# One fused attention, expert and feed-forward kernel: when two weight matrices are converted, and how the second layer's first product sits in PSUM

## The chip, the cores and the metric

The kernel runs on one core of a Trainium2 chip. The metric is device microseconds (us) of that core from start to end of the program. A core has TensorE (matmuls, called PE in the profile, with its weight loads as PEld), VectorE (DVE), ScalarE (ACT), GpSimd (POOL) and SyncE (SP, which here only issues DMAs). SBUF is the on-chip working memory; PSUM, where matmuls write, has eight banks of 2 KB per partition.

## The reference

Three stages follow each other. The test data are random draws.

```python
# 1. attention, 2 batches x 8 heads, 768 positions, 64 wide: scores only within equal cluster
mask = q_assign[:, :, :, None] == k_assign[:, :, None, :]      # nearest centroid of 16, per head
scores = np.where(mask, 0.125 * (q @ k.T), -1e9)
x = softmax(scores) @ v                                        # -> 1536 tokens x 512
# 2. mixture of experts, 8 experts, one expert per token: the first layer
e_idx = np.argmax(x @ w_gate + modality_bias[modality_id], axis=1)
h = np.maximum(x[mask] @ w1[e], 0.0)                           # 512 -> 1024
out[mask] = gate_w[mask, None] * (h @ w2[e])                   # 1024 -> 512
# 3. dense feed-forward: the second layer
h = x @ w_in                                                   # 512 -> 2048, w_in is float64
g = h * np.tanh(log1p(exp(h)))                                 # mish
return (g @ w_out).astype(np.float32)                          # 2048 -> 512, w_out is float64
```

## The kernel before

Every product is made of three float16 matmuls (high by high, high by low, low by high part), so each operand must be split in a high and a low float16 part. [...] One chunk (`conv_chunk`, L1021 to L1035) is a 512 KB load, three integer operations on VectorE that shift the bits of a double into those of a float (L1027, L1028, L1030), one ScalarE copy to float16 (L1033), and one VectorE operation for the low part (L1035). `convs` (L1039) does the 16 chunks as a generator of steps: six empty ones, then four for each chunk, after the third of which it issues the load of the chunk after next (two load buffers, `RAWB`).

The program is written as such generators: `attention()` for the 16 heads, `moe1()` for the first layer (`M`), `gate(0)` and `gate(1)` for routing and sorting the tokens of a batch, `convs("i")` and `convs("o")`, `h_units(q)` and `o_units(q)` for the first and second product of the second layer over a sixth of the tokens (a third of one batch, 256 tokens). The first layer takes each batch in two slots (the two most common experts), and each slot in eight pieces: four of `w1`, whose results are `hT` (L963 to L969), four of `w2`, whose results are `x1` (L978 to L993). `h_units` needs `x1` of its batch and `win`; `mish` (L1095) turns four of its 16 column blocks at a time into `g` (ScalarE: sigmoid, arctan, sin; VectorE multiplies by the product that still lies in PSUM, L1110; ScalarE and GpSimd split the result, L1113 and L114); `o_units` needs `g` and `wout`.

While attention is emitted, steps of the other generators are put between its steps: from step 163 on, one step of `convs("i")` at every second one (`CI1 = 2`, L1302), unless batch 0 is being gated, and the first layer at a set pace (L1307). Then what is left of `convs("i")` is emitted at once (L1315). After that three calls of `mix` share out the rest: `mix` always takes a step of the part that has done the smallest fraction of the length it is given. The first mix (L1328) has the second slot of batch 0, `gate(1)` with a length of 40, the first 20 steps of `convs("o")` and `h_units(0)`; the second (L1329) the first slot of batch 1, `h_units(1)` and all the rest of `convs("o")`; the third (L1331) the last slot, and all products that remain.

A scheduler then orders the instructions of PE, DVE, ACT and POOL by its own estimate of times, within what the data allow; each engine executes its list in order. SyncE's list is kept in the order in which the program is written. So every load that SyncE issues stands behind the wait of the load before it.

In PSUM the second layer's first product has two tiles of two banks, each holding four column blocks (`h_t[q]`, L1131); its second product has two tiles of a bank, and two banks are shared by the rest.

## Time and profile before

| | us |
|---|---|
| median of 3 runs (689.56 to 696.43) | 689.66 |
| the profiled execution | 697.58 |
| its span, first to last instruction | 695.9 |
| PE busy, share of the span | 616.7, 89% |
| DVE busy | 400.6, 58% |
| ACT busy | 459.3, 66% |
| POOL busy | 294.9, 42% |

Shares over the whole span hide the stages. The profile is read in stretches, and their limits are events: the twelfth head's output leaves VectorE at 233.0, the sixteenth's at 320.6; the first `hT` after attention is done at 324.0, the last `x1` of batch 1's first slot at 451.6; the last matmul ends at 687.8. A matmul's end is modelled, and PE counts as busy while short matmuls overlap, so busy PE is not PE at its peak. A VectorE record overlaps the next by some 0.08 us; busy times count that once.

### The profile page before, as it was taken

How to read it: one execution, taken by the hardware profiler on the slowest of the kernel's cores; microseconds unless marked ns; L12 is line 12 of the kernel's file. 1: busy time of each engine (PE TensorE's matmuls, PEld its weight loads, DVE VectorE, ACT ScalarE, POOL GpSimd, SP SyncE). 2: the span in 40 equal slices, each digit the busy share in tenths (PEclk: the TensorE clock that was granted, in tenths of full speed). 3: DMA queues.
4: the chain of work that ended last, by engine and by line, in shares of the span. 5: the costliest groups of instructions: out<-in, count | busy, mean ns of one | idle time of the engine just before them, and what ended most of it. 6: DMA issues, size and time to landing. Idle time of an engine off the chain costs nothing.

```text
span 695.9 us, 14026 instructions
## 1 busy us (share of the span) xinstructions
PE 616.7 (89%) x5618; PEld 409.6 (59%) x5619; DVE 400.6 (58%) x751; ACT 459.3 (66%) x699; POOL 294.9 (42%) x251
## 2 busy tenths in 40 slices
PE   1698999987589988987999889999999999999995
PEld 1365867756356645554766556666666667667542
DVE  6768767689699899999858888823121110110100
ACT  2587998875678767765677678846554476776500
POOL 5577888796776744551141211111311212313211
PEclk9999999989789999999999999999999999999999
DMA  7532372312853234346445544321100000000000
GB/s 229 139 74 64 87 206 53 87 41 61 273 162 102 68 97 121 123 128 189 135 158 183 183 150 161 113 61 31 47 16 1 15 16 1 31 1 31 2 31 34
DMA packets 56743, 64.43 MB, mean 93 GB/s; under 512 B 10080, under 2 KB 46944, under 8 KB 56672
## 3 DMA queue, kind: packets, MB, share of 16 engines
q1 hardware_dynamic: 42064, 48.74, 24.1%
q10 hardware_dynamic: 12688, 8.42, 4.0%
q0 software_dynamic: 1920, 6.32, 2.4%
q8 instruction: 46, 0.75, 0.5%
q14 instruction: 25, 0.20, 0.1%
HBM read 46.23 MB, written 6.32 MB: 76 GB/s over the span
## 4 chain that ended last, share of the span: by engine, by line
PE 40%; DVE 28%; issue 10%; ACT 9%; DMA 7%; SPq 3%; POOL 1%; ACTq 0%; POOLq 0%; DVEq 0%
PE h L1007 12%; PE o L1159 12%; PE eps L1007 6%; DVE f L1028 4%; DVE mxh L351 3%; DVE f L1030 3%; PE s L391 2%; DVE w L922 2%; DMA QK<-hl 2%; DVE f L1027 2%; DMA QK<-oT 2%; DVE win L1035 2%; DVE mxh L356 1%; DVE dg L702 1%; PE eps L273 1%
## 5 line engine op out<-in xcount | busy, mean ns | idle before, releaser
L114 POOL TENSOR_TENSOR el<-e,eh 128x768 f16<-128x768 f32 x86 | 146.0, 1709 | 63.9 <-ACT eh L400 42.9
L1007 PE MATMUL h<-x,win 128*128 128x256 f16 x1152 | 133.3, 273 | 3.2 <-ACT s L1103 2.4
L1007 PEld LDWEIGHTS <-win 128*128 128x128 f16 x1152 | 112.5, 98 | 24.1 <-issue 4.7
L1110 DVE SCALAR_TENSOR_TENSOR s<-s,h 128x1024 f32<-128x1024 f32 x24 | 29.3, 1222 | 167.4 <-ACT s L1108 164.8
L1007 PEld LDWEIGHTS <-w 128*128 128x128 f16 x768 | 75.2, 99 | 67.6 <-issue 12.1
L114 POOL TENSOR_TENSOR xb<-s,xb 128x1024 f16<-128x1024 f32 x18 | 39.6, 2201 | 142.7 <-ACT xb L1113 142.5
L1159 PE MATMUL o<-wout,xb 128*128 128x512 f16 x432 | 96.8, 379 | 0.0
L391 PE MATMUL s<-QK 128*128 128x384 f16 x320 | 80.2, 346 | 9.6 <-ACT e L393 9.2
L393 ACT ACTIVATE e<-s 128x384 f32<-128x384 f32 x152 | 70.0, 489 | 24.5 <-PE s L391 19.3
L1007 PE MATMUL eps<-xw,w 128*128 128x416 f16 x384 | 76.8, 349 | 8.7 <-DVE hT L969 3.2
L400 ACT ACTIVATE eh<-e 128x768 f16<-128x768 f32 x88 | 74.3, 848 | 2.5 <-PE s L391 1.3
L351 DVE TENSOR_REDUCE mxh<-x 128x1 f32<-128x512 f32 x96 | 64.6, 680 | 17.2 <-PE x L350 17.1
L1103 ACT ACTIVATE s<-h,cst 128x512 f32<-128x512 f32 x48 | 32.8, 686 | 61.8 <-PE h L1007 61.5
L1007 PE MATMUL eps<-hT,w 128*128 128x416 f16 x384 | 71.6, 339 | 0.7 <-DVE hT L969 0.7
L1159 PEld LDWEIGHTS <-xb 128*128 128x128 f16 x432 | 42.3, 98 | 47.6
L429 PE MATMUL av<-vst,el 128*128 128x65 f16 x528 | 61.3, 197 | 5.8 <-POOL el L114 5.8
L427 PE MATMUL av<-vst,eh 128*128 128x65 f16 x528 | 63.8, 198 | 1.9 <-DVE xt L442 1.6
L428 PE MATMUL av<-vst,eh 128*128 128x64 f16 x528 | 63.8, 199 | 0.0
L429 PEld LDWEIGHTS <-el 128*128 128x128 f16 x528 | 51.3, 102 | 15.5 <-POOL el L114 11.3
L427 PEld LDWEIGHTS <-eh 128*128 128x128 f16 x528 | 51.5, 100 | 9.1 <-DVE xt L442 2.6
L391 PEld LDWEIGHTS <-QK 128*128 128x128 f16 x384 | 35.3, 103 | 33.3 <-issue 20.6
L428 PEld LDWEIGHTS <-eh 128*128 128x128 f16 x528 | 51.4, 101 | 3.3 <-issue 0.3
(224 smaller groups left out, 1053.4 us busy)
## 6 DMA issues: line engine op xcount, KB each, us to landing
wf<-in_moe_w_dram ACTq DMA_DIRECT2D x16, 512.0 KB
raw<-in_moe_w_in_dram SPq DMA_DIRECT2D x16, 512.0 KB
raw<-in_moe_w_out_dram SPq DMA_DIRECT2D x16, 512.0 KB
wf<-in_moe_w_dram SPq DMA_DIRECT2D x16, 512.0 KB
QK<-hl SPq DMA_DIRECT2D x32, 192.0 KB
xs<-dr SPq DMA_DIRECT2D x12, 258.0 KB
t<-in_k_dram SPq DMA_DIRECT2D x8, 384.0 KB
t<-in_q_dram SPq DMA_DIRECT2D x8, 384.0 KB
```

Of the source, the lines that this page charges most:

```text
L114: nc.gpsimd.tensor_tensor(out=out_, in0=in0, in1=in1, op=ALU.subtract)
L351: nc.vector.reduce_max(out=mx_t[i][:, t, 0:1], in_=sp, axis=AX.X)
L391: nc.tensor.matmul(sps[hf][:, 0:HS], lhsT=st[:, KA + a, kt * P:(kt + 1) * P], rhs=st[:, QA + a, hf * HS:(hf + 1) * HS], start=(a == 0), st ...
L393: nc.scalar.activation(out=e32[:, hf * HS:(hf + 1) * HS], in_=sps[hf][:, 0:HS], func=AF.Exp, scale=1.0 / float(D) ** 0.5)
L400: nc.scalar.activation(out=eh, in_=e32, func=AF.Copy)
L427: nc.tensor.matmul(av[:, t, :], lhsT=eh[:, cols], rhs=vs[:, h, 0:NV], start=(kt == 0 and t == 0), stop=False, skip_group_check=True)
L428: nc.tensor.matmul(av[:, t, 0:D], lhsT=eh[:, cols], rhs=vs[:, h, NV:], start=False, stop=False, skip_group_check=True)
L429: nc.tensor.matmul(av[:, t, :], lhsT=el[:, cols], rhs=vs[:, h, 0:NV], start=False, stop=(kt == T - 1), skip_group_check=True)
L1007: nc.tensor.matmul(out_, lhsT=wc[:, a, kk, ms], rhs=mv[:, c, kk, :], start=(i == 0), stop=(i == n - 1))
L1103: nc.scalar.activation(out=s[:, u:u + hf], in_=pt[:, u:u + hf], func=AF.Sigmoid, scale=2.0 ** -17, bias=cst[:, 1:2])
L1110: nc.vector.scalar_tensor_tensor(out=s, in0=s, scalar=2.0 ** -6, in1=pt, op0=ALU.mult, op1=ALU.mult)
L1159: nc.tensor.matmul(pts[t], lhsT=gsl[q % 2][f // FB][:, f % FB, a, t * P:(t + 1) * P], rhs=wout[:, c, f, :], start=(f == 0 and i_ == 0), st ...
```

## The change

Five things change.

- The steps of `convs("i")` go between attention's steps at every fourth place instead of every second (`CI1`). What is left is no longer emitted in one piece: it opens the conversions' part of the first mix.
- The first two mixes become one: the second slot of batch 0 and the first slot of batch 1 in a row, `gate(1)` with a length of 90, the rest of `convs("i")` followed by 26 steps of `convs("o")`, and `h_units(0)` and `h_units(1)` in a row. The rest of `convs("o")` goes into the last mix, with a length of 320 (`CVF` times 64).
- `h_units` and `o_units` hold back a product in the emitted order until its chunk's conversion has been emitted (`cv_done`).
- The first product's tiles are four of one bank instead of two of two. `mish` takes the list of tiles, and the multiplication L1110 becomes two of 512 columns.
- The loop for tokens of rarer experts (`rest`), which makes no trips on these data, is adapted to the new tiles.

```diff
-    CV1 = 20
+    CV1 = 26
-    CI1 = 2
+    CI1 = 4
+    CVF = 5.0
-    GA = 40.0
+    GA = 90.0
...
+    cv_done = set()
...
             for _ in ch:
                 pass
+            cv_done.add((nm, j))
             yield 1.0
...
-    def mish(pt, gg, q, k, n=FB, w_=QW):
+    def mish(pts, gg, q, k, w_=QW):
         m2 = m_p["m2"]
+        n, m = gg.shape[1], pts[0].shape[1]
         s = m2.tile([P, FB, QW], F32, tag="s", name="s", bufs=3)[:, 0:n, 0:w_]
-        hf = max(n // 2, 1)
-        for u in range(0, n, hf):
-            nc.scalar.activation(out=s[:, u:u + hf], in_=pt[:, u:u + hf], func=AF.Sigmoid, scale=2.0 ** -17, bias=cst[:, 1:2])
-            if u + hf < n:
+        for u in range(n // m):
+            if u:
                 yield
                 yield
+            nc.scalar.activation(out=s[:, m * u:m * (u + 1)], in_=pts[u], func=AF.Sigmoid, scale=2.0 ** -17, bias=cst[:, 1:2])
...
-        nc.vector.scalar_tensor_tensor(out=s, in0=s, scalar=2.0 ** -6, in1=pt, op0=ALU.mult, op1=ALU.mult)
+        for u, pt in enumerate(pts):
+            su = s[:, m * u:m * (u + 1)]
+            nc.vector.scalar_tensor_tensor(out=su, in0=su, scalar=2.0 ** -6, in1=pt, op0=ALU.mult, op1=ALU.mult)
...
-            while q > 1 and (q - 2, f // 4) not in o_done:
+            while ("i", f) not in cv_done or q > 1 and (q - 2, f // 4) not in o_done:
                 yield None
             if f % FB == 0:
-                h_t[q] = m_p["ps"].tile([P, FB, QW], F32, tag="h", name="h", bufs=2)
-            mm3(h_t[q][:, f % FB], win, x1[:, :, :, p * QW:(p + 1) * QW], CD, slice(f * P, (f + 1) * P))
+                h_t[q] = []
+            if f % 2 == 0:
+                h_t[q].append(m_p["ps"].tile([P, 2, QW], F32, tag="h", name="h"))
+            mm3(h_t[q][-1][:, f % 2], win, x1[:, :, :, p * QW:(p + 1) * QW], CD, slice(f * P, (f + 1) * P))
...
         for f4 in range(NF // 4):
+            while ("o", 4 * f4 + 3) not in cv_done:
+                yield None
...
-    for _ in CI:
-        pass
+    cv_left = 4.0 * (NCV - sum(k_[0] == "i" for k_ in cv_done))
...
-    mix([m_until(0, 1), 2 * C1 - m_done[0]], [gate1(), GA], [part(CV, CV1), float(CV1)], [h_units(0), CH])
-    mix([m_until(1, 0), C1], [h_units(1), CH], [CV, 4.0 * NCV + 6 - CV1])
+    mix([seq(m_until(0, 1), m_until(1, 0)), 3 * C1 - m_done[0]], [gate1(), GA], [seq(CI, part(CV, CV1)), cv_left + CV1], [seq(h_units(0), h_units(1)), 2 * CH])
-    mix([m_until(1, 1), C1 / FM], [ho, 10 * CH])
+    mix([m_until(1, 1), C1 / FM], [ho, 10 * CH], [CV, CVF * 4.0 * NCV])
```

Line numbers of the changed kernel are higher by 1 up to L1036 and by up to 10 after it; L1116 there is L1110 here.

VectorE's list at the end of attention (`xt` is the output of the sixteenth head, `x` the first layer's result `x1`, `w` the low part of an expert's weights, `f` the chunk under conversion). Before:

```order
L1027 TENSOR_SCALAR f_5672<-raw 128x512
L440 TENSOR_SCALAR r<-av 128x6
L1028 SCALAR_TENSOR_TENSOR f_5672<-raw,f_5672 128x512
L441 RECIPROCAL r<-r 128x6
L1030 SCALAR_TENSOR_TENSOR f_5672<-raw,f_5672 128x512
L442 TENSOR_TENSOR xt<-av,r 128x384
L991 SCALAR_TENSOR_TENSOR x_4251<-eps,x_4251 128x416
L922 SCALAR_TENSOR_TENSOR w<-wf,w 128x1024
L1035 SCALAR_TENSOR_TENSOR win<-f_5672,win 128x4x128
L969 SCALAR_TENSOR_TENSOR hT<-eps,hT 128x416
```

And after:

```order
L441 TENSOR_SCALAR r<-av 128x6
L442 RECIPROCAL r<-r 128x6
L443 TENSOR_TENSOR xt<-av,r 128x384
L992 SCALAR_TENSOR_TENSOR x_4251<-eps,x_4251 128x416
L923 SCALAR_TENSOR_TENSOR w<-wf,w 128x1024
L970 SCALAR_TENSOR_TENSOR hT<-eps,hT 128x416
L474 COPY xT<-x 128x768
```

The chunk that stood among these rows is the fourteenth of `win` (its first three operations and its last); eight chunks stand ahead of this place in the changed kernel, and none among them.

VectorE's list where the first layer finishes the second slot of batch 0 (`xw` are sorted tokens of batch 1, `tm` a strip of `x1`). Before:

```order
L1027 TENSOR_SCALAR f_6324<-raw 128x512
L991 SCALAR_TENSOR_TENSOR x_4251<-eps,x_4251 128x352
L993 SCALAR_TENSOR_TENSOR tm<-eps,tm 128x64
L1028 SCALAR_TENSOR_TENSOR f_6324<-raw,f_6324 128x512
L922 SCALAR_TENSOR_TENSOR w<-wf,w 128x1024
L1030 SCALAR_TENSOR_TENSOR f_6324<-raw,f_6324 128x512
L720 SCALAR_TENSOR_TENSOR xw<-o,xw 128x4x128 x2
L1035 SCALAR_TENSOR_TENSOR wout<-f_6324,wout 128x512
```

And after:

```order
L1028 TENSOR_SCALAR f_5974<-raw 128x512
L923 SCALAR_TENSOR_TENSOR w<-wf,w 128x1024
L1029 SCALAR_TENSOR_TENSOR f_5974<-raw,f_5974 128x512
L1031 SCALAR_TENSOR_TENSOR f_5974<-raw,f_5974 128x512
L721 SCALAR_TENSOR_TENSOR xw<-o,xw 128x4x128
L992 SCALAR_TENSOR_TENSOR x_4251<-eps,x_4251 128x352
L994 SCALAR_TENSOR_TENSOR tm<-eps,tm 128x64
L1036 SCALAR_TENSOR_TENSOR win<-f_5974,win 128x4x128
L1028 TENSOR_SCALAR f_6146<-raw 128x512
```

Here the third chunk of `wout` was under way before; in the changed kernel it is the ninth of `win`, the next of which follows at once.

SyncE's list, from the last heads' rows on (`QK` are the heads' operands, `xs` the sorted rows of batch 1 that come back from memory, `ei` the experts' numbers, `wf` the experts' weights of batch 1). Before:

```order
L303 DMA QK_119<-oT 32x2x192 x4
L1019 DMA raw<-in_moe_w_in_dram 128x4x128 x2
L303 DMA QK_120<-oT 32x2x192 x4
L1019 DMA raw<-in_moe_w_in_dram 128x4x128 x12
L1019 DMA raw<-in_moe_w_out_dram 128x512 x2
L832 DMA xs<-dr 128x1032 x2
L1019 DMA raw<-in_moe_w_out_dram 128x512
L832 DMA xs<-dr 128x1032 x4
```

And after:

```order
L1020 DMA raw<-in_moe_w_in_dram 128x4x128 x2
L304 DMA QK_119<-oT 32x2x192 x4
L304 DMA QK_120<-oT 32x2x192 x4
L1020 DMA raw<-in_moe_w_in_dram 128x4x128 x6
L833 DMA xs<-dr 128x1032 x2
L1020 DMA raw<-in_moe_w_in_dram 128x4x128 x3
L833 DMA xs<-dr 128x1032 x4
L1020 DMA raw<-in_moe_w_in_dram 128x4x128
```

Ten loads of `w_in` now stand ahead of the first `xs`, where all sixteen and two of `w_out` stood; the other six come between and behind the `xs` and the `wf`.

## Rows read from the trace of the kernel before

**Rows 1.** Windows view: busy us of each engine (count), granted clock, DMA.
```profile
core 0: us, PE busy (x) PEld busy (x) DVE busy (x) ACT busy (x) POOL busy (x), PEclk, DMA share, GB/s
100.00:150.00 50.00, 44.94 (x622) 33.69 (x621) 37.23 (x79) 40.90 (x77) 42.06 (x38) 0.97 0.33 86
233.00:324.00 91.00, 77.00 (x837) 49.38 (x836) 84.06 (x117) 63.09 (x112) 45.95 (x29) 0.96 0.41 125
250.00:260.00 10.00, 7.85 (x46) 3.90 (x45) 8.75 (x17) 6.10 (x13) 5.21 (x4) 0.83 0.17 54
270.00:280.00 10.00, 7.47 (x89) 5.07 (x88) 9.32 (x16) 8.20 (x17) 6.73 (x5) 0.83 0.41 117
324.00:393.00 69.00, 64.33 (x512) 45.12 (x511) 53.90 (x134) 48.69 (x67) 18.14 (x14) 1.00 0.52 168
393.00:452.00 59.00, 55.62 (x362) 35.75 (x362) 48.80 (x65) 46.17 (x58) 6.77 (x3) 0.97 0.44 143
452.00:600.00 148.00, 148.00 (x985) 96.17 (x984) 26.74 (x32) 86.73 (x101) 31.07 (x21) 1.00 0.07 22
```

**Rows 2.** Waits of PE between 233 and 324: us in total, times, longest.
```profile
PE s L391 <- ACT e L393: 3.2, 3, 1.8
PE av L429 <- POOL el L114: 2.5, 2, 1.5
PE eps L1007 <- DVE l L486: 2.2, 1, 2.2
PE eps L1007 <- DVE x L991: 1.7, 1, 1.7
PE eps L1007 <- DVE xT L473: 1.3, 1, 1.3
PE x L350 <- DVE mxh L351: 1.0, 1, 1.0
```

**Rows 3.** Costliest groups of VectorE, 233 to 324: busy us, mean ns.
```profile
L1030 DVE SCALAR_TENSOR_TENSOR f<-raw,f 128x512 int32<-128x512 int32 x12 | 15.5, 1295 | 0.2
L1028 DVE SCALAR_TENSOR_TENSOR f<-raw,f 128x512 int32<-128x512 int32 x12 | 14.1, 1173 | 0.2
L1035 DVE SCALAR_TENSOR_TENSOR win<-f,win 128x512 f16<-128x512 f32 x13 | 13.4, 1028 | 2.8 <-ACT win L1033 2.8
L1027 DVE TENSOR_SCALAR f<-raw 128x512 int32<-128x512 int32 x13 | 8.4, 648 | 0.4 <-DMA raw<-in_moe_w_in_dram 0.2
```

**Rows 4.** The same operations, 324 to 452.
```profile
L922 DVE SCALAR_TENSOR_TENSOR w<-wf,w 128x1024 f16<-128x1024 f32 x16 | 20.2, 1262 | 0.2 <-ACT w L918 0.2
L1028 DVE SCALAR_TENSOR_TENSOR f<-raw,f 128x512 int32<-128x512 int32 x18 | 19.3, 1075 | 0.3
L1030 DVE SCALAR_TENSOR_TENSOR f<-raw,f 128x512 int32<-128x512 int32 x18 | 12.4, 686 | 0.3
L1035 DVE SCALAR_TENSOR_TENSOR wout<-f,wout 128x512 f16<-128x512 f32 x16 | 11.0, 688 | 4.9 <-ACT wout L1033 4.8
L1110 DVE SCALAR_TENSOR_TENSOR s<-s,h 128x1024 f32<-128x1024 f32 x8 | 9.8, 1221 | 14.4 <-ACT s L1108 11.9 <-issue 2.5
L969 DVE SCALAR_TENSOR_TENSOR hT<-eps,hT 128x416 f16<-128x416 f32 x16 | 9.4, 584 | 1.1 <-ACT s L1103 1.1
L1027 DVE TENSOR_SCALAR f<-raw 128x512 int32<-128x512 int32 x18 | 7.6, 422 | 1.6 <-DMA raw<-in_moe_w_out_dram 1.4
L720 DVE SCALAR_TENSOR_TENSOR xw<-o,xw 128x512 f16<-128x512 f32 (+2 forms) x7 | 4.0, 605 | 1.0 <-ACT xw L717 1.0
```

**Rows 5.** Waits of PE between 324 and 452.
```profile
PE eps L1007 <- DVE hT L969: 3.5, 4, 2.1
PE h L1007 <- ACT s L1103: 2.4, 4, 1.2
PE h L1007 <- DVE s L1110: 0.8, 1, 0.8
```

**Rows 6.** Chain that ended last, behind 455: start us, us, what.
```profile
462.63 2.62 PE h L1007 x24
465.25 2.59 PE o L1159 x12
467.84 2.11 PE eps L1007 x12
```

More of the change, by code (lines that the diff above doesn't have):

```diff
@@ L1037, in clustered_attention_moe_kernel @@
     NCV = 16
+    assert NCV == NF
+    cv_done = set()
     def convs(nm):
@@ L1222, in rest @@
                 for f in range(NF):
-                    pt = ps2.tile([P, 1, P], F32, tag="h", name="h", bufs=2)
+                    pt = ps2.tile([P, 1, P], F32, tag="h", name="h")
                     mm3(pt[:, 0], win, x1, CD, slice(f * P, (f + 1) * P))
-                    for _ in mish(pt, gsl[0][f // FB][:, f % FB:f % FB + 1, :, 0:P], None, f, 1, P):
+                    for _ in mish([pt], gsl[0][f // FB][:, f % FB:f % FB + 1, :, 0:P], None, f, P):
                         pass
```

## The prediction

> **What bounds the kernel now.** I read the windows view first, since the shares of the whole span mix stages. Behind 452 PE is busy for 148.00 of 148 us, and in the chain of waits its matmuls follow each other without a gap, at 0.109 us for one of the second layer's first product (2.62 / 24), 0.216 for one of its second (2.59 / 12) and 0.176 for one of the first layer (2.11 / 12) [rows 1, 6]. Nothing that leaves PE's work alone shortens that part. All that can be won lies ahead of it, where PE idles: 14.0 us between 233 and 324, when the last four heads and the first slot run, and 4.7 + 3.4 us from there to 452 [rows 1].
>
> In the first of these stretches VectorE is busy for 84.06 of 91 us, 92% [rows 1]. The waits view says what PE waits for: of the 14.0 us, 2.2, 1.7, 1.3 and 1.0 are ended by VectorE, 3.2 and 2.5 by ScalarE and GpSimd [rows 2]. The groups of VectorE's work show the cause: the conversion's four operations lead it, with 15.5 + 14.1 + 13.4 + 8.4 = 51.4 us of the 84 [rows 3]. Two slices of 10 us have a granted clock of 0.83 [rows 1], which is part of the time at the lower of two levels (1.2 of 2.4 GHz), in slices where PE is busy for only 7.85 and 7.47 us; they cost 2 x 0.17 x 10 = 3.4 us. From 324 to 452 VectorE has 78% and then 83%, and PE is near its limit with 93% and 94% [rows 1].
>
> **The change, part by part.** *Fewer chunks beside attention.* VectorE's list had 13 chunks of `win` end between the twelfth head's output and the first `hT` behind attention; the changed list has 8. A chunk there costs 0.648 + 1.173 + 1.295 + 1.028 = 4.14 us [rows 3], so 5 x 4.14 = 20.7 us leave, and VectorE keeps 84.1 - 20.7 = 63.4. It is then no longer the bound; PE is, with 77.0 us of busy time. In the next stretch, with VectorE at 78%, PE is busy for 64.33 of 69, 93.2% [rows 1]; at that share 77.0 takes 82.6. The 3.4 us of clock I count as returned, since that stretch has 1.00, so 79.2 for 91: **11.8 won**. VectorE would then stand at 63.4 / 79.2 = 80%, close to the 78% I started from. Bounds: nothing, if the heads' own chain holds (attention alone, 100 to 150, has PE at 44.94 of 50 [rows 1]), and 14.0 + 3.4 = 17.4, if PE never waits.
>
> *The same chunks, later.* From 324 to 452 PE's work stays the same: 384 matmuls of the first product and 372 of the first layer. VectorE gets 15 chunks (8 of `win`, 7 of `wout`) for 18. A chunk costs 0.422 + 1.075 + 0.686 + 0.688 = 2.87 us there [rows 4], which would be a gain of 8.6 us of VectorE, but they stand closer together: none until the first column block of the second slot's `x1`, and then nine until the eighth `mish` multiplication, where the list of PE has 96 x 0.109 + 132 x 0.176 + 58 small ones at half of 0.109 = 37 us. VectorE's other work is (53.9 + 48.8 - 18 x 2.87) / 128 = 0.40 us per us [rows 1, 4]. At its 92%, the stretch lasts T with 0.92 T = 25.8 + 0.40 T, so 50 us: PE loses 12 to 13 there. The other 78 us of PE's work in this part have few chunks and take some 80. Together 129.6 for 128: **1.6 lost**. Bounds: 8 won (no idle time left) and, at 4.14 us for each of the nine chunks, 9 x 1.27 / 0.52 = 22 lost.
>
> *The rest of `w_out` beside the last mix.* Nine chunks, 25.8 us, go beside the next 50 us of PE. VectorE has 26.74 / 148 = 18% there [rows 1], so it comes to 70%. At 78% PE idled 6.8%, at 18% nothing: **1.5 lost**, bounds 0 and 3.4. Second products that need these chunks stand behind them in the list by at least a group of four.
>
> *The loads.* SyncE's list had twelve loads of `w_in` and two of `w_out` ahead of the first `xs`; now six, and the others go between the `xs` and the `wf` of batch 1. A load waits until VectorE has emptied its buffer, and the `wf` behind it wait too. `wf` are asked for three pieces ahead (L946); a piece is at least 24 matmuls of 0.176, so 12 us cover a wait for a chunk of 3 to 4 us. I count nothing; if that cover is gone, it is the third rival.
>
> *One bank per tile.* 24 multiplications of 1.221 become 48 of half the size. Another operation with 512 columns from PSUM has 0.605 (forms with fewer columns among them) [rows 4], so the price is about 0 to 3 us of VectorE over 300 us, hidden where VectorE is idle 80% of the time. What it can win is PE's waits for the product's tiles, 2.4 + 0.8 us [rows 5]; between 0 and 3.2 I take **0.5**, as a bank comes free by half an operation, 0.6 us, sooner and most of these waits are for the sigmoid and not for the multiplication.
>
> Sum: 11.8 - 1.6 - 1.5 + 0.5 = 9.2 won. The profiled execution of 697.58 would come to 688.4. It lies 7.9 above the median of 689.66; nothing shows where these 7.9 are, so I take the same 9.2 from the median: **680.5**.
>
> **A rule against the flat price.** What decides over the second term is whether a moved chunk costs 4.14 or 2.87. The bit operations L1030 have a mean of 1295 ns beside attention and 686 ns behind it [rows 3, 4], with GpSimd busy for 45.95 of 91 and 18.14 of 69 [rows 1]. So I price by the stretch in which a chunk lands. The Trainium skill, "SBUF — State Buffer", section "Who interferes with whom", gives a reason: a VectorE instruction with two SBUF inputs and a GpSimd instruction that reads SBUF exclude each other for their whole length, whichever issues first. The rows agree with that. By a price without this rule, 4.14 everywhere, the sum would be 9.2 - 22 + 1.6, a loss of 11.
>
> **The rivals.** *Attention's own chain takes over* (20%). For it: with VectorE at only 37.23 of 50, attention alone keeps PE at 90%, with ScalarE and GpSimd at 82 and 84% [rows 1]; 5.7 of the 14.0 us of waits are already ended by these two [rows 2]. Then 77.0 at 90% takes 85.6, and with no clock returned the first term is 5.4; with the losses of 1.6 and 1.5 some 2.3 are won: 687. Against it: beside the last heads these two have only 69% and 50%.
>
> *PE fills up* (20%). The first term goes to its bound of 17.4 and the moved chunks fit into what VectorE has free, so the second and third cost nothing: 17.9 won, 672. For it: each wait that VectorE ended also delayed the exponentials that PE waits for next. Against: none of the stretches before 452 [rows 1] has PE above 94%.
>
> *Just in time is too late* (11%), the slower one. PE executes in order, so a first product that waits for its chunk holds up the first layer behind it, whose outputs stand in VectorE's list between the chunks. The place is the nine chunks between the second slot's first `x1` and the eighth multiplication, with `wf` loads behind the `raw` loads on SyncE. At 4.14 us a chunk costs 22 there, and the same price beside the last mix 9 x 1.27 = 11 of VectorE on 35 of 50, some 3 more of PE's time: 11.8 - 22 - 4.5 + 0.5 = 14 lost, at the bound, and 7 to 8 halfway into it: 697 at the price of about 3.8. It decides from where a chunk costs 3.3 us: there 9 x 0.45 / 0.52 = 8 eat what is left of the gain. For it: L1028 has 1075 ns even behind attention [rows 4], so blocking goes on. Against: GpSimd has 26% and 11% there [rows 1].
>
> That nothing moves is no rival: the lists show eight chunks where thirteen were.
>
> **How the numbers follow.** The forecast has 49%, its own range is 675 to 686; the rivals have 20% (687), 20% (672) and 11% (697). The range for 8 in 10 leaves out the slow case and the far ends of the others: **670 to 690**. About 1%, 6.9 us, is what a measurement of this kernel can tell from no change, so the limits are 682.8 and 696.6. Faster by more: the fuller recovery, 20%, and three quarters of the forecast, 37%, so 57%. Slower by more: 10%. Within: 33%.
>
> **What would show it.** Right: attention's last output some 12 us sooner than 320.6, VectorE at 80% or less before it, a granted clock of 1.00 there, the first `hT` behind it near 312; then PE's idle time gathered around the second slot's `x1`, 10 us or more, L1030 still near 690 ns there; no idle PE from about 490 on. The second term is wrong where PE shows waits of several us for L1035 (`win`), the load term where it waits through `w` for `wf`. The whole is wrong where attention ends as late as before: then its own chain was the bound and VectorE only busy beside it.

## The result and the profile after

The changed kernel takes **699.39 us** (median of 20 runs, 694.98 to 702.12) for 694.53 of the kernel before, measured beside it (20 runs too): ratio **1.0071**, interval 1.0048 to 1.0093. Measured again later it was 696.65 for 693.75, ratio 1.0049, interval 1.0022 to 1.0076. So it is 3 to 5 us slower; 680.5 had been forecast, in 670 to 690. The profiled execution took 700.66, its span is 699.0, its granted clock 0.959 (before: 697.58, 695.9, 0.971).

The windows of the changed kernel that answer to [rows 1], same columns:

```profile
233.00:324.00 91.00, 80.85 (x849) 51.25 (x848) 68.69 (x101) 60.39 (x105) 44.78 (x29) 0.91 0.27 84
324.00:393.00 69.00, 61.67 (x473) 41.84 (x472) 54.07 (x127) 43.88 (x62) 17.07 (x13) 1.00 0.55 172
393.00:452.00 59.00, 52.45 (x353) 35.48 (x351) 43.09 (x56) 44.38 (x55) 8.94 (x4) 0.91 0.42 138
452.00:600.00 148.00, 148.00 (x982) 95.97 (x981) 53.51 (x79) 93.76 (x110) 30.43 (x19) 1.00 0.15 48
```

VectorE falls from 84.06 to 68.69 us in the first stretch (63.4 had been forecast), but PE gains only 3.85 us of busy time there, and in this trace its granted clock falls from 0.96 to 0.91; in a second trace of the same kernel, below, the clock is 0.96 there, as before. In the next two stretches PE is busy for 61.67 + 52.45 = 114.1 us for 120.0 before, with a clock of 0.91 for 0.97 in the second. Behind 452 nothing is lost, with VectorE's time doubled.

Cut at 290, the first stretch shows where VectorE's relief went. The kernel before:

```profile
250.00:290.00 40.00, 33.69 (x348) 21.07 (x347) 37.77 (x55) 28.48 (x52) 21.20 (x14) 0.91 0.30 90
290.00:320.00 30.00, 24.71 (x255) 15.57 (x254) 27.57 (x34) 18.20 (x31) 13.74 (x8) 1.00 0.49 151
```

and the changed one:

```profile
250.00:290.00 40.00, 29.85 (x341) 19.14 (x338) 37.22 (x48) 27.94 (x51) 20.43 (x12) 0.87 0.26 80
290.00:320.00 30.00, 30.00 (x275) 18.41 (x274) 13.07 (x19) 16.67 (x28) 12.60 (x8) 0.94 0.25 80
```

Up to 290 the chunks did not thin out: VectorE is as full as before there (37.22 of 40, third busy column), and behind 290 it stands half empty. PE won 5.3 us behind 290, where it now never idles, and lost 3.8 ahead of it.

**The first hole.** A "hole" is here a place where PE's short waits lie close together. From the timeline of the changed kernel (start, duration, then the idle time before and what ended it):

```profile
264.29 1.68 POOL L115 TENSOR_TENSOR el<-e,eh 128x768 f16<-128x768 f32 x1 [2.28 <-ACT eh L401]
264.38 2.67 DVE L923 SCALAR_TENSOR_TENSOR w<-wf,w 128x1024 f16<-128x1024 f32 x1
266.97 0.68 DVE L352 TENSOR_REDUCE mxh<-x 128x1 f32<-128x512 f32 x1
267.70 0.38 PE L351 MATMUL x<-QK 128*128 128x512 f16 x1 [1.74 <-DVE mxh L352]
268.29 0.63 ACT L1034 ACTIVATE win<-f 128x512 f16<-128x512 f32 x1 [3.75 <-DVE f L1031]
...
269.35 0.68 PE L392 MATMUL s<-QK 128*128 128x384 f16 x2 [0.78 <-ACT e L394]
270.57 3.42 POOL L115 TENSOR_TENSOR el<-e,eh 128x768 f16<-128x768 f32 x2 [4.60 <-ACT eh L401]
...
272.56 1.98 DVE L1029 SCALAR_TENSOR_TENSOR f<-raw,f 128x512 int32<-128x512 int32 x1
274.26 1.77 POOL L115 TENSOR_TENSOR el<-e,eh 128x768 f16<-128x768 f32 x1 [0.28 <-POOL el L115]
274.57 2.01 DVE L1031 SCALAR_TENSOR_TENSOR f<-raw,f 128x512 int32<-128x512 int32 x1
276.50 0.55 DVE L443 TENSOR_TENSOR xt<-av,r 128x384 f32<-128x384 f32 x1
277.10 0.24 PE L428 MATMUL av<-vst,eh 128*128 128x65 f16 x1 [2.32 <-DVE xt L443]
```

VectorE's `w` operation starts beside GpSimd's subtraction and takes 2.67 us; a maximum of attention (`mxh`) stands behind it, and PE waits 1.74 for that. ScalarE has waited 3.75 for the chunk's third bit operation, with attention's exponentials behind the copy, and PE waits for those (0.78). Then two bit operations take 1.98 and 2.01 us beside GpSimd, the head's output `xt` stands behind them, and PE waits 2.32. PE had idled for 1.74 and 0.78 us when the granted clock fell: it is 0.98 in 260 to 270 and 0.51 in 270 to 280, so nearly all of the second slice is at the lower of the two levels, 1.2 of 2.4 GHz.

**The second hole**, from the same view (`L1119` splits a result of `mish`):

```profile
410.26 2.13 POOL L115 TENSOR_TENSOR xb<-s,xb 128x1024 f16<-128x1024 f32 x1 [21.78 <-ACT xb L1119]
410.74 1.93 DVE L1028 TENSOR_SCALAR f<-raw 128x512 int32<-128x512 int32 x1
412.36 2.31 POOL L115 TENSOR_TENSOR gx<-s,gx 128x1024 f16<-128x1024 f32 x1
413.10 2.11 DVE L1029 SCALAR_TENSOR_TENSOR f<-raw,f 128x512 int32<-128x512 int32 x1
415.24 0.69 DVE L1031 SCALAR_TENSOR_TENSOR f<-raw,f 128x512 int32<-128x512 int32 x1
415.97 0.63 ACT L1034 ACTIVATE wout<-f 128x512 f16<-128x512 f32 x1 [2.00 <-DVE f L1031]
...
422.53 0.62 ACT L1034 ACTIVATE wout<-f 128x512 f16<-128x512 f32 x1
423.05 1.04 ACT L1119 ACTIVATE xb<-s 128x1024 f16<-128x1024 f32 x1
423.99 0.51 ACT L966 ACTIVATE hT<-eps 128x416 f16<-128x416 f32 x1
424.55 0.51 PE L1008 MATMUL eps<-hT,w 128*128 128x416 f16 x1 [3.94 <-ACT hT L966]
```

ScalarE stands still for 2.00 us for a chunk of `w_out` whose bit operations run slowly beside GpSimd. What is queued behind its copy, sigmoids and the rest up to the second copy at 422.53 and one more operation, goes first, and the first layer's `hT` gets its turn at 423.99. PE, in order, waits 3.94 us, and 1.50 more for the next `hT` behind a bit operation of 2.50 us. In windows, the kernel before first, then the changed one:

```profile
420.00:430.00 10.00, 10.00 (x77) 7.32 (x75) 8.81 (x11) 7.65 (x11) 2.39 (x1) 1.00 0.43 148
430.00:440.00 10.00, 10.00 (x68) 6.39 (x67) 9.19 (x13) 8.71 (x10) 2.07 (x1) 1.00 0.63 200
```

```profile
420.00:430.00 10.00, 4.56 (x23) 2.70 (x22) 8.04 (x10) 7.40 (x10) 2.14 (x1) 0.66 0.00 0
430.00:440.00 10.00, 10.00 (x60) 6.35 (x59) 7.38 (x12) 7.75 (x9) 0.80 (x1) 0.83 0.60 210
```

### The profile page after: what moved, and what is told of

Same layout as the page of the kernel before. It is cut to its first block, busy times and chain, and to the rows that moved or that the text cites. A ratio compares the mean times of both kernels' runs of the same rounds, so it can differ in the third digit from the quotient of the medians.

```text
span 699.0 us, 14072 instructions
## 1 busy us (share of the span) xinstructions
PE 616.7 (88%) x5618; PEld 410.0 (59%) x5619; DVE 406.0 (58%) x775; ACT 458.7 (66%) x697; POOL 295.6 (42%) x251
## 5 line engine op out<-in xcount | busy, mean ns | idle before, releaser
L1008 PE MATMUL h<-x,win 128*128 128x256 f16 x1152 | 134.9, 275 | 3.6 <-ACT win L1034 2.6
L1116 DVE SCALAR_TENSOR_TENSOR s<-s,h 128x512 f32<-128x512 f32 x48 | 30.8, 684 | 132.6 <-ACT s L1112 132.6
L1008 PE MATMUL eps<-hT,w 128*128 128x416 f16 x384 | 75.4, 349 | 11.0 <-DVE hT L970 6.3
L351 PE MATMUL x<-QK 128*128 128x512 f16 x96 | 37.8, 399 | 14.5 <-DVE mxh L352 11.4
```

Of the source, the lines that this page charges most:

```text
L351: nc.tensor.matmul(sp, lhsT=st[:, QA, t * P:(t + 1) * P], rhs=st[:, KA, 0:512], start=True, stop=True)
L1008: nc.tensor.matmul(out_, lhsT=wc[:, a, kk, ms], rhs=mv[:, c, kk, :], start=(i == 0), stop=(i == n - 1))
L1116: nc.vector.scalar_tensor_tensor(out=su, in0=su, scalar=2.0 ** -6, in1=pt, op0=ALU.mult, op1=ALU.mult)
```

## The experiments

All ratios are to the kernel before, measured beside the variant; the variants were measured in five groups, each with its own runs of the kernel before. "PE" is its busy time in a window of the trace, and there is one trace of each variant. "Expected" texts count idle time of PE higher than the windows view has it (12.8 us between 260 and 290 in the changed kernel, for 30 - 21.55 = 8.5); the windows view is what is compared here. Every edit makes the scheduler plan all lists anew, so an edit in one place can move instructions in another.

**The split of the banks.** The kernel before with only the new `mish` and `h_units` tiles:

```
+            if f % 2 == 0:
+                h_t[q].append(m_p["ps"].tile([P, 2, QW], F32, tag="h", name="h"))
```

> The kernel before with one part of the change alone: each PSUM bank of the second layer's first product is a tile of its own (48 multiplications of some 0.68 us for 24 of 1.22); the conversions stay where they were. Theory A (the loss is made by where the conversions stand, the split is neutral): ratio to before 0.997 to 1.003, that is 0 to 2 us either way, and no PE wait of over 2 us at a single place between 400 and 450. Theory B (the split costs, since two multiplications and their two waits stand in VectorE's list for one): ratio 1.005 to 1.009, the whole difference of 4.9 us between the two kernels.

694.09 us, ratio 1.0009, interval 0.998 to 1.0039. The split costs nothing that can be measured; what the changed kernel loses comes from the rest of the change.

**How many chunks beside attention.** The changed kernel with a step after every second step of attention, and then after every one (`CI1 = 1`):

```
-    CI1 = 4
+    CI1 = 2
```

> The changed kernel with one part undone: a step of the w_in conversion again after every second step of attention (13 chunks beside attention, 3 behind it), the rest as changed. If thinning out the chunks beside attention is worth what the traces suggest (attention's last product 3.0 us sooner), this is slower than the changed kernel by 2 to 4 us in the stretch up to the second slot's end, and gives back part of it later since 5 chunks fewer stand before the products: ratio to before 1.003 to 1.010. If instead the loss of the changed kernel is made by chunks just ahead of the first product (5 more of w_in between 350 and 400 push those of w_out into the third slot), it is faster than the changed kernel by 4 us or more: ratio 1.000 or less.

687.92 us, ratio **0.9925**, interval 0.9893 to 0.9956: faster than both kernels. In its trace twelve chunks end beside attention and four behind it (13 and 3 had been expected). Attention's last output is at 312.9, in the changed kernel at 313.61 + 0.56 = 314.2.

> The changed kernel with a step of the w_in conversion after every step of attention: 15 chunks end beside attention, one behind it. With 13 there the run before this one was 11 us faster than the changed kernel (8 there) and attention ended no later. Theory A2 (a chunk beside attention costs nothing, since its own chain leaves VectorE time; a chunk that the first product of slot 0 waits for costs PE some 2 us): attention's last product stays at 311 to 313 us, and three chunks fewer behind it give up to 5 us more: ratio to before 0.985 to 0.993. Theory D (VectorE, at 92% with 13 chunks, is full): attention ends 8 us or more later (3 chunks of 4.14 us in the span that is left), and the ratio is 0.998 or more.

695.78, ratio 1.0012 (0.9982 to 1.0043): the theory that a chunk beside attention costs nothing fell. With 14 there attention's last output is at 323.9, 3 to 11 us later than in the traces with twelve or 13 (312.9; 320.6 before; 315.6 in the bank-split kernel, whose list is the same there).

**What VectorE's work beside attention costs.** The kernel before, its 13 chunks there without the sign and the low bits:

```
+        if not (key[0] == "i" and key[1] < 13):
             nc.vector.scalar_tensor_tensor(out=fi, ... scalar=-(1 << 30), ...)
...
+        if not (key[0] == "i" and key[1] < 13):
             nc.vector.scalar_tensor_tensor(out=fi, ... scalar=29, ...)
```

> The kernel before, but the 13 w_in chunks beside attention leave out two of their five operations (the sign and the low three bits, L1028 and L1030 in it), some 26 x 1.1 = 29 us of VectorE beside the last heads; everything else stays. The forecast's first term (VectorE at 84 of 91 us is the bound there) expects attention's last product some 11 us sooner, and a ratio of 0.985 or less. Theory A2 (VectorE is busy there and not the bound) expects attention's last product within 3 us of 311 to 316, and a ratio of 0.996 to 1.002.

683.78, ratio 0.9857 (0.9811 to 0.9903). The forecast's reading holds here: with 26 operations fewer attention's last output is at 309.9, against 320.6 and 315.6, and all 16 chunks have ended by then, where 13 had. VectorE's work does cost time in this stretch. (From the eleventh head's output, ahead of the first chunk's end, to the sixteenth's it is 94.8 us, against 101.0 and 99.7; the rest of the 10.7 us lies before that.) So the question became why removing whole chunks did not pay.

**Number or order.** The changed kernel with the same cut on its eight chunks beside attention (`key[1] < 8`), the kernel before with its line `CI1 = 2` made 4 and nothing else, and the changed kernel with `CI1 = 3`:

> The changed kernel, but the eight w_in chunks beside attention leave out two of their five operations (the sign and the low three bits, L1029 and L1031; 16 operations, some 20 us of VectorE between 231 and 295). The same cut on the 13 chunks of the kernel before gave 10 us. Theory G (the eight chunks of the changed kernel stand as close together as before, 7 us apart between 254 and 290, and make the hole of PE between 260 and 280 with its 10.2 us at half of the clock): PE's idle time there and the half clock at 270 go, ratio falls from 1.007 to 0.999 or less. Theory H (the hole has another cause, attention's own chain or the expert weights' w operations): ratio 1.004 or more, the hole stays.

692.15, ratio 0.9972 (0.9946 to 0.9998); PE 27.13 of 30 from 260 to 290, for 21.55, with VectorE at 12.65 for 27.35. Without this work there is no hole there.

> The kernel before with the pace beside attention alone changed: a step of the w_in conversion after every fourth step of attention, and the chunks that are left (7 or 8) at once behind attention, as before, with no product waiting for single chunks. If the loss of the changed kernel comes from fewer chunks beside attention and more behind it, however they are placed there, this loses too: ratio 1.004 to 1.012. If it comes from holding back products for single chunks (just in time), this keeps what the thinning was worth: ratio 0.998 or less. If neither matters alone, 0.998 to 1.004.

697.52, ratio 1.0054 (1.0035 to 1.0072). The slower pace alone makes a loss of this size, and the first hole comes with it, at the same place. But it did not thin out the chunks as expected: what is emitted at once behind attention was planned into its last heads, so that 13 chunks end beside attention, as before, and VectorE is busy for 28.13 of 30 us from 290 to 320. The number is the old one; the order of the list is new. Its window at the hole:

```profile
260.00:290.00 30.00, 21.67 (x243) 14.01 (x242) 27.29 (x36) 20.41 (x38) 15.19 (x10) 0.83 0.33 100
```

> The changed kernel with a step of the w_in conversion after every third step of attention. VectorE's list then keeps the chunks beside the first of the last heads where the kernel before has them (10 or 11 there) and none beside the last two, where the kernel before had four to five. Theory G (the hole between 260 and 280 belongs to the list that a step after every fourth makes): the hole is gone as in the runs with a step after every second; with 2 or 3 chunks more behind attention than in the run at 0.9925, some 2 us each: ratio 0.996 to 1.001. Theory A2 alone (only the count of chunks behind attention matters): 3/5 of the way from 0.9925 to 1.007, ratio 1.001. A lottery of the planned order would give anything from 0.992 to 1.008.

689.09, ratio 0.9916 (0.9886 to 0.9945), PE 24.12 of 30 there with a clock of 1.00, though only nine chunks stand beside attention and seven behind it, one less than in the changed kernel. So the number of chunks does not make the first hole.

Counting the steps from one later keeps the eight chunks and plans another list:

```
-        if na > NA0 and na % CI1 == 0 and ...
+        if na > NA0 and na % CI1 == 1 and ...
```

> The changed kernel with the w_in conversion's steps beside attention counted from one step of attention later (same pace, same eight chunks beside attention, eight behind it). The planned order comes out otherwise: the expert layer's first outputs and the first chunk stand one head later against each other, as in the runs paced after every second or third step. If the order makes the hole of PE between 260 and 290: its idle time there is 7 to 8 us for 12.8, no half clock of 10 us at 270, ratio 0.992 to 1.001. If the number of chunks (eight beside attention, eight behind it) makes the loss: hole or not, ratio 1.004 or more.

692.62, ratio **0.998** (0.995 to 1.001), against 1.0049 (1.0022 to 1.0076) for the changed kernel in the same group. Its windows, and two `w` operations of VectorE in its timeline:

```profile
250.00:290.00 40.00, 33.52 (x370) 21.93 (x369) 36.46 (x54) 28.75 (x54) 20.01 (x13) 0.96 0.30 93
290.00:320.00 30.00, 30.00 (x299) 19.23 (x298) 15.79 (x29) 19.37 (x32) 11.31 (x8) 1.00 0.29 90
```

```profile
254.85 1.23 DVE L923 SCALAR_TENSOR_TENSOR w<-wf,w 128x1024 f16<-128x1024 f32 x1 [0.16 <-ACT w L919]
...
265.93 1.22 DVE L923 SCALAR_TENSOR_TENSOR w<-wf,w 128x1024 f16<-128x1024 f32 x1
```

The same eight chunks, and no hole: PE does 63.5 us of work in these 70 for 58.4 before, and keeps what thinning gives behind 290. The `w` operations meet no subtraction and take 1.2 us. The 4 us between the two medians (696.65 and 692.62) cannot be put to the first hole alone, though: the list behind attention is another one too. From 380 to 460 PE's wait of 3.9 us for ScalarE's `hT` is gone and the clock is 1.00, for 0.94.

**Does the hole recur?** The changed kernel as it is:

> The changed kernel as it is, for a second trace and on the same chip as its variants: ratio 1.004 to 1.010. If its two holes are made by the order of its instructions, PE idles 12 to 13 us again between 260 and 290 and 10 or more between 380 and 460, with a stretch of 10 us at half of the clock near 270 and one near 423. If the clock falls by chance, these stretches lie elsewhere.

696.65, ratio 1.0049. Its windows, and PE's longest waits from 380 to 460:

```profile
260.00:290.00 30.00, 21.49 (x244) 13.78 (x243) 27.32 (x35) 19.97 (x37) 15.23 (x10) 0.89 0.23 72
...
380.00:460.00 80.00, 71.20 (x480) 48.17 (x481) 62.83 (x83) 54.69 (x70) 14.07 (x6) 0.94 0.44 144
```

```profile
PE eps L1008 <- ACT hT L966: 3.9, 1, 3.9
PE eps L1008 <- DVE hT L970: 3.2, 3, 1.5
```

Both holes are where they were (21.55 and 71.02 in the first trace), with the same waits to 0.1 us, and so are the slow operations: the `w` takes 2.66 us, the bit operations 1.98 and 2.01. The clock follows less closely: near 270 it is at the lower level for 6.8 us in two pieces, not for 10.2 in one, and over 233 to 324 it is 0.96.

**The second hole.** All copies on VectorE (the new line without its condition), and only those behind attention:

```
+        if "wout" in m_p:
+            nc.vector.tensor_scalar(out=dst[:, 0], in0=ff, scalar1=64.0, ...)
+        else:
             nc.scalar.activation(out=dst[:, 0], in_=ff, func=AF.Copy, scale=64.0)
```

> The changed kernel with the conversion's copy to the high half taken off ScalarE's list and put into VectorE's (32 operations of 0.6 to 0.7 us more on VectorE, 20 us in all; ScalarE no longer waits for the third bit operation). Theory A (ScalarE, in order, stands behind this wait, 3.75 us before 268.29 and 2.0 us before 415.97 in the changed kernel, and with it the exponentials and the first-layer outputs that PE waits for): both waits go, PE's half-clocked stretches of 10.2 us at 269.5 and 423.1 too, and the kernel is 4 to 8 us faster than the changed one: ratio to before 0.996 to 1.001. Theory D (VectorE's time itself is the bound, wherever it is spent): 20 us more of it make it slower than the changed kernel by 3 us or more: ratio over 1.011.

693.05, ratio 1.002 (0.9988 to 1.0053). The second hole went (PE 76.31 of 80 from 380 to 460), while from 260 to 290 PE has 20.87 of 30, against the expectation. Taking the copy off ScalarE does not close the first hole; with VectorE now busy for 29.66 of these 30 us, it may also be another hole in the same place.

> The changed kernel with the conversion's copy on VectorE for the chunks behind attention alone (8 of w_in, 16 of w_out); beside attention nothing changes. Theory A (behind attention ScalarE's wait for the third bit operation holds up the first-layer outputs that PE waits for): PE's idle time between 380 and 460 falls from 13 us to 6 or 7, the half clock of 10.2 us at 423 goes, the hole between 260 and 290 stays: ratio 0.998 to 1.002, 4 to 6 us under the changed kernel. If the gain of the run with all copies moved came from the copies beside attention: ratio 1.005 or more.

695.66, ratio 1.0025 (0.9998 to 1.0051). Window and waits:

```profile
380.00:460.00 80.00, 75.64 (x517) 50.54 (x515) 69.91 (x99) 54.09 (x64) 13.25 (x6) 0.98 0.49 157
```

```profile
PE eps L1008 <- DVE x L992: 3.3, 2, 2.3
PE eps L1008 <- DVE hT L970: 0.7, 1, 0.7
```

PE's wait for ScalarE's `hT` is gone and PE has 4.4 to 4.6 us more of work done there. In time it gives 1 us on the changed kernel of the same group, within both intervals: the mechanism is shown, its price is not well measured.

The same cut of two operations on the late chunks of `w_in` (`key[1] >= 8`) instead:

> The changed kernel, but the eight w_in chunks behind attention leave out two of their five operations (the sign and the low three bits, L1029 and L1031; 1.16 + 0.70 us each in the changed kernel, 15 us of VectorE); where they stand and what waits for them stays. Theory A2 (PE waits for these chunks and for the first-layer outputs between them, so their length is paid almost in full): slot 0 of the second layer ends 10 us sooner than 394 us, and the ratio falls from 1.007 to 0.995 or less. Theory F (it is not the chunks' length but their order, ScalarE's copy ahead of other work and the products held back until the next chunk is there): at most 4 us, ratio 1.001 or more.

692.79, ratio 0.998 (0.9955 to 1.0005): 0.7 to 0.9% for 16 operations, between the two theories' limits. PE has 73.37 of 80 with a clock of 1.00 in 380 to 460.

**How late `w_out` may come.** The changed kernel with all of it in the first mix, and then with `CI1 = 2` and `CV1 = 6`, all in the last:

```
-    CV1 = 26
+    CV1 = 70
```

> The changed kernel with all of the w_out conversion in the first mix, at that mix's pace, none in the last one. Theory A (each chunk that stands between the third slot's first-layer outputs costs, as the wait of 3.94 us before 424.55 shows): with more chunks in the same stretch it is slower than the changed kernel by 3 us or more, ratio to before over 1.011. Theory C (the loss comes from moving w_out chunks behind 450 or from pacing them there): faster than the changed kernel by 2 us or more, ratio 1.004 or less.

709.43, ratio 1.0224 (1.0181 to 1.0267), 10 us or more over the changed kernel. PE has 51.90 of 60 from 320 to 380, for 55.09, and 70.83 of 80 behind it.

> The changed kernel with the w_in conversion beside attention as before (13 chunks) and no chunk of w_out ahead of the last mix, so all 16 of w_out stand beside it. Theory A2 (chunks between the first-layer outputs cost PE 1.4 us each, as the run with all of w_out in the first mix showed: 10 us for 7): seven fewer there give 3 to 8 us on the same kernel with w_out paced as changed: ratio to before 0.981 to 0.988. Rival E (the products of the second half then wait for w_out chunks, and first products for the buffers that these free): PE waits behind 440, and the ratio is 0.993 or more.

696.53, ratio 1.004 (1.0008 to 1.0071). That is the rival: second products now wait for their chunks, as PE's one group of waits from 440 to 500 says:

```profile
PE o L1169 <- ACT wout L1034: 5.8, 3, 2.8
```

**Joining the remedies** (the copy's edit with `CI1 = 2`, with `CI1 = 3`, and with the count from one step later), and `CI1 = 3` again:

> The fastest kernel so far (the changed one with the w_in conversion paced beside attention as before, ratio 0.9925) with the conversion's copy moved from ScalarE to VectorE as in the run that gained 0.5% on the changed kernel. Theory A (ScalarE's wait for the third bit operation is a cost of its own, wherever the chunks stand): 2 to 5 us faster still, ratio 0.985 to 0.990. If VectorE is short beside attention with 13 chunks there (20 us more on it, 10 of them beside attention), it loses 3 us or more: ratio 0.997 or more.

692.26, ratio 0.9974 (0.9954 to 0.9994): no gain, and the second of the two expectations; it has a hole of its own between 260 and 290 (PE 19.20 of 30, VectorE 29.59).

> A step of the w_in conversion after every third step of attention (0.9916 with nothing else changed) and the conversion's copy on VectorE for the chunks behind attention alone. If the two places are independent and both cost, 2 to 4 us faster than the first alone (its PE idles 6.2 us between 380 and 460, some 2 more than the best run there): ratio 0.986 to 0.990. If the planned order decides, which changes with every edit, anything from 0.988 to 1.000.

692.18, ratio 0.9987 (0.9953 to 1.002), PE 21.05 of 30 from 260 to 290: edits behind attention planned the chunks beside it anew.

> The changed kernel with both remedies: steps of the w_in conversion beside attention counted from one step later, and the copies of the chunks behind attention on VectorE. If the two places are separate causes their gains add, 0.998 of the one less the 0.2 to 0.5% that the other gave: ratio 0.991 to 0.997, with 5 to 8 us of idle PE between 260 and 290 and 4 to 7 between 380 and 460. If the second edit plans the chunks beside attention into another order with a hole of its own, PE idles 10 us or more between 260 and 290 and the ratio is 0.998 or more.

692.51, ratio 1.0 (0.9973 to 1.0026), PE 21.71 of 30: the second edit brought a hole back there.

> The kernel with a step of the w_in conversion after every third step of attention once more (0.9916 before, interval 0.9886 to 0.9945): ratio 0.989 to 0.996 if that was no accident of its call; PE idle 7 to 8 us between 260 and 290 and 0 to 1 between 290 and 320 again.

692.06, ratio 0.9983 (0.9957 to 1.0009), PE 25.84 and 29.89 of 30. So the same kernel has 0.9916 in one group and 0.9983 in another; differences of half a per cent between groups are not read here. The 0.9925 of `CI1 = 2` was not repeated. It and `CI1 = 3` are the best found; neither has the first hole.

## Why the prediction was wrong

Of the 18.9 us between 680.5 and 699.39 some 5 lie in the base: the median of three runs was 689.66, that of the twenty beside the changed kernel 694.53. The other 14 are in the terms: 9.2 won was the forecast, 4.9 were lost.

The first two terms were priced between events, so the traces can be cut at the same events: from the twelfth head's output to the first `hT` behind attention, and from there to the last `x1` of batch 1's first slot. The lists put a little more or less of PE's work into a stretch, so the second number of each pair is the time beyond it: the length less the columns of the matmuls that ended in it, at 0.216 us for 512 [rows 6].

| trace | first stretch, beyond PE's work | second stretch, beyond PE's work |
|---|---|---|
| before | 91.0, 23.4 | 127.6, 13.2 |
| forecast | 79.2 | 129.6 |
| before, banks split | 89.6, 22.0 | 127.9, 13.3 |
| changed | 86.4, 20.6 | 135.1, 20.6 |
| changed, second trace | 84.0, 18.2 | 135.2, 20.4 |
| counted one step later | 80.3, 14.3 | 137.1, 19.4 |
| late copies on VectorE | 84.7, 18.9 | 132.4, 14.2 |
| all copies on VectorE | 82.3, 18.0 | 132.6, 14.4 |
| `CI1 = 3`, two traces | 81.3, 15.3 and 79.3, 13.3 | 132.2, 17.0 and 134.3, 17.4 |
| `CI1 = 2` | 86.0, 19.5 | 124.8, 9.2 |

So the first term won 2.8 and 5.2 us in the two traces (1.4 less against the split-bank trace), for 11.8, and the second lost 7.4 and 7.2, for 1.6. Both steps failed; the sum of what they gave, 2 to 5 us lost, is about the measured difference. And the chunks behind attention do cost there: with four of `w_in` instead of eight (`CI1 = 2`) the second stretch has 9.2.

**First term, 11.8 won: the relief spread over the whole stretch.** "at that share 77.0 takes 82.6" takes PE's share as even over 91 us. VectorE came to 75% of the stretch (80% or less had been forecast), and the run with thinned chunks shows that its work there does cost time. But the planned list takes the eight chunks at the old spacing, six of them from 254 to 291, and the five that left had stood beside the last heads. Where they left PE won its 5.3 us. Where they stayed, the new list put a `w` operation and two bit operations beside GpSimd's subtractions, just ahead of values that PE waits for: the hole, 4 us of busy time. The clock of 1.00 that I counted on did not come either: it is 0.91 in one trace and 0.96, as before, in the other. Where the list has no hole (the run counted one step later), the stretch gives 9.1 us, so most of the 11.8 was there to be won. That the measured 2.8 and 5.2 lie near the first rival's 5.4 is luck: its mechanism, attention's own chain, is not what ends the waits in the hole.

**Second term, 1.6 lost: a wrong mechanism.** A chunk there costs (changed kernel, 324 to 452, busy us and mean ns)

```profile
L1029 DVE SCALAR_TENSOR_TENSOR f<-raw,f 128x512 int32<-128x512 int32 x15 | 17.4, 1158 | 0.2
L1031 DVE SCALAR_TENSOR_TENSOR f<-raw,f 128x512 int32<-128x512 int32 x15 | 10.4, 695 | 0.4
L1028 DVE TENSOR_SCALAR f<-raw 128x512 int32<-128x512 int32 x16 | 10.2, 637 | 2.8 <-DMA raw<-in_moe_w_out_dram 2.5
L1036 DVE SCALAR_TENSOR_TENSOR wout<-f,wout 128x512 f16<-128x512 f32 x7 | 4.8, 688 | 3.3 <-ACT wout L1034 3.3
```

0.637 + 1.158 + 0.695 + 0.688 = 3.18 us, not far above the 2.87 I took. But I let PE lose what overfills VectorE, and VectorE is at 78% and 73%. In the place where I put the loss, from the second slot's first `x1` to the eighth multiplication (356.5 to 406.8), the changed kernel takes the 50 us of the forecast, but PE is busy for 44.8 of them, not 37. The loss lies behind it, in the second hole: 5.4 us of idle time and a clock of 0.66 and 0.83 between 420 and 440, where the kernel before has 20 of 20 and 1.00. PE's waits between 324 and 452 that are new or longer, beside the 3.9 us for ScalarE's `hT`:

```profile
PE eps L1008 <- DVE hT L970: 5.6, 5, 2.0
PE h L1008 <- ACT win L1034: 2.6, 3, 1.4
```

In the account of the change I counted what a chunk costs VectorE, never what its copy holds up on ScalarE. ScalarE waits for third bit operations about as long as before in this stretch, 25.2 us for 24.5; what stands behind the copy is new, an `hT` that PE needs next. With the late copies on VectorE, in two kernels, 6 of the 7 us are gone from the stretch, though the median of the one measured beside the changed kernel gains only 1 us. The sum had a slip as well: beside the 37 us, 83 of PE's 119.95 are left, not 78, and at the same pace the term would have been near 7 lost. That this is the measured size is luck, since the place and the wait are others.

**Third term, 1.5 lost:** nothing; PE is busy for 148.00 of 148. With all of `w_out` there (and `CI1 = 2`) it would be 5.8 us of waits. **Loads, 0:** right as far as PE shows: none of its waits is ended by a DMA, and ScalarE's part of `w` waits for `wf` for 0.6 us in all between 324 and 452. **Banks, 0.5 won:** no difference measured; 48 multiplications of 684 ns for 24 of 1221.

**The rivals.** The slower one, 697, had the right sign and half of the mechanism: just in time does hold up the first layer's outputs. It decided "from where a chunk costs 3.3 us", and 3.18 was measured. But it put the loss among the chunks of `w_in` ahead of the first product, whose waits came to 2.6 + 0.3 us only, and its 7 to 8 us of loss stand for 4.9 measured. Its 11% was too little, since I let one average decide over two stretches that are decided by a few collisions. No rival had the hole beside attention.

**The clock.** In the later group the mean granted clock is 0.972 before and 0.965 after; in the first it is 0.961 after. (1 - clock) x time is then 19.8 us before, 24.2 and 27.0 after: 4 to 7 us more. That is no separate loss to be added, since part of it lies where PE waits anyway. From the thirteenth head's output to the fourteenth's, around the first hole, both traces of the changed kernel take 23.8 us, with 10.2 us at the lower level near 270 in one and 6.8 in the other (20.2 us before, 18.9 counted one step later). The forecast priced the clock in the first stretch alone. The lower level is no cause of its own there: in both traces of the changed kernel most of it, between 233 and 452, lies at the two holes, and in the run without the first hole the clock from 260 to 290 is 1.00.

**Left open.** Which of the collisions makes the first hole was not isolated: no edit tried here changes one instruction and leaves the other lists as they are. A collision by itself makes none: in the kernel before a `w` operation of 2.66 us (at 297.01) and bit operations of 2.02 (at 279.68 and 284.25) stand too. What each hole costs in the medians was not measured apart from the other.

## What to carry to other kernels

A stretch's busy share says that an engine is short, not where its relief will land: cut the stretch at the places from which work really leaves in the new list, and price only those. Afterwards cut the traces at events, not at fixed times, and take off the work that was moved. Work that is moved just ahead of its use carries its whole chain with it; ask of each engine on that chain, not of the busiest alone, what stands behind the step that waits. Where a planner orders the lists, try the same change under a few neutral shifts before judging it: here one step of phase moved the median by 4 us, as much as the whole change.

## What the runs showed of the hardware

The same list gives the same collisions: in two executions of the changed kernel, in different groups, the slow operations agree to 0.01 us (2.67 and 2.66; 1.98 and 1.98; 2.01 and 2.01), while spans differ by 3 us and the clock's stretches lie differently. VectorE's bit operation with one input, L1028, has 0.43 us alone (at 262.93) and 1.93 beside a subtraction of GpSimd; the `w` operation 1.22 alone and 2.67 when it starts 0.09 us behind one of 1.68. That 2.67 is close to 1.68 + 1.22 - 0.09 = 2.81. The Trainium skill, "SBUF — State Buffer", section "Who interferes with whom", says that a VectorE instruction with two SBUF inputs, as the `w` operation is, contends with a GpSimd instruction that reads SBUF. Of VectorE's two-port modes, which it says `tensor_scalar` can enter, it says that whoever issues first has the shared ports for the whole instruction and the other blocks. The rows agree with both.
